# Two heads' scores in single tiles, and unused matmuls in TensorE's waits, at the start of an attention and feed-forward kernel

## The chip, the cores and the metric

The kernel runs on one core of a Trainium2 chip. A core has five engines that run side by side and meet through semaphores: TensorE (PE, matrix products; PEld is its weight load), VectorE (DVE), ScalarE (ACT), GpSimd (POOL) and SyncE (SP), which here only issues transfers. The metric is the time of one execution on the device, in microseconds (us), lower is better. "Before" was run five times: median 357.24, from 355.94 to 357.76.

## The reference

Attention over 8 batches of 8 heads with 576 positions of width 64, then a feed-forward layer. Sixteen beacon keys and values stand ahead of the 576 of each head; every query sees all beacons, and the keys up to its own position.

```python
k_all = np.concatenate([beacon_k, k], axis=2)      # (8, 8, 592, 64)
v_all = np.concatenate([beacon_v, v], axis=2)
scores = scale * np.matmul(q, k_all.transpose(0, 1, 3, 2))
scores = np.where(causal, -1000000000.0, scores)
a = np.exp(scores - scores.max(-1, keepdims=True))
a /= a.sum(-1, keepdims=True) + 1e-09
attn_out = np.matmul(a, v_all)
x = attn_out.transpose(0, 2, 1, 3).reshape(B * S, H * D)   # (4608, 512)
h = x @ w_in                                               # (4608, 2048)
out = np.maximum(0.01 * h, h) @ w_out                      # (4608, 512)
```

## The kernel before, in words

**Pairs.** Heads are worked on two at a time: a pair `g` is batch `g // 4`, heads `2 * (g % 4)` and the next, so there are 32 pairs. For a pair the kernel needs queries and keys transposed (`qT`, `kT`, 128 partitions: two heads of 64), makes the scores as keys by queries in four tiles (`score(g, 0)` to `score(g, 3)`, L286), each followed by one exponential on ScalarE (L306) that writes `aT`, sets the masked part of `aT` to zero on GpSimd (`masks`, L310, four instructions), multiplies by the values (`value(g, 0)` and `value(g, 1)`, L332; a column of ones beside the values gives the sum to divide by), and turns the result (`x_transposes`, L368) into `xT`, where it waits for the second stage. Score tiles have two PSUM buffers of their own (`ps_sc`), so the third tile waits for the first one's exponential. Everything else in PSUM shares four buffers (`ps_one`).

**Two ways to get qT and kT.** Pairs 0 to 7, the first two batches, are transposed by TensorE (`t_q(g, 0)` for queries, `t_q(g, 1)` for keys, L228: 18 transposes each, then a copy, on VectorE or, where the call says so, on ScalarE). The pair after is always prepared while a pair is worked on. From pair 8 on GpSimd reorders the raw data (`permute`, L157), a transposing DMA turns it (`turn_pairs`, L257, issued by SP), and GpSimd copies it in order into `qT` and `kT` (`in_order`, L269 to L282; the copies are L277).

**Second stage.** Rows of `x` are taken in 9 chunks of 512. `moe1` (L382) makes one of 16 tiles of `h` with four matmuls of 512 columns and a leaky ReLU on ScalarE; `moe2` (L398) makes a quarter of an output tile of 128 rows, also four matmuls; every fourth one ends in a copy to `osb` on VectorE and a store issued by SP (L420). `fill()` (L425) emits one such unit, `moe1` or `moe2` by turns, when a chunk is ready. Units are put between the steps of attention so that TensorE has work.

**Transfers.** SP issues the values (`load_v`, L206, six transfers per batch) and the stores; GpSimd issues queries, keys and weights (`load_qk`, `load_w_in`, `load_w_out`). The very first pair is loaded in float32 by SP and ScalarE (`load_first_pair`, L144) and cast by VectorE (queries, L471) and ScalarE (keys, L472). Values are cast to bfloat16 by GpSimd (`cast_v`, L221).

**Order.** The order of instructions on each engine is written out by hand: within `tc.manual_schedule` (L451) every engine executes in the order of the program, and waits in that order. So the loop at L534 is the schedule: in step `g` come `loads(g)`, then, for the first eight pairs (L538 to L562), two score tiles, the transposes of an earlier pair's result, the transposes for the pair to come, the first half of an earlier pair's values, two score tiles, second half, masks. Step 8 (L564) brings the loads of batch 2, the rest of pairs 5 to 7 and a run of 22 units; from there each step has a number of units worked out from what is left (L591 to L597). Before all this `warm_up(34)` (L440, called at L477) issues 34 matmuls of the identity with itself, whose result nobody reads, while the first loads are under way.

Of the kernel before, what the change touches and what calls it, by code (L numbers as in the profile page):

```python
# [8 lines left out]
FP32 = mybir.dt.float32  # L9
# [6 lines left out]
def kernel(  # L16
# [11 lines left out]
    nc = tc.nc  # L28

    B, H, S, D = q.shape  # L30
# [5 lines left out]
    NPAIR = H // 2  # L36
# [41 lines left out]
    ps_one = ctx.enter_context(tc.tile_pool(name="ps_one", bufs=4, space=bass.MemoryType.PSUM))  # L78
# [3 lines left out]
    ident = singles.tile([128, 128], BF16, name="ident")  # L82
# [59 lines left out]
    first_raw = []  # L142
# [78 lines left out]
    def cast_v(b, eng, c0=0, c1=NKB):  # L221
        t, dst = v_raws[b], v_bufs[b % 2]
        for c in range(c0, c1):
            eng.tensor_copy(out=dst[0 : ROWS[c], c, :, 0:D], in_=t[0 : ROWS[c], c])  # L224
# [212 lines left out]
            turn[0] = 0  # L437
        return can1 or can2

    def warm_up(n):  # L440

        ps = ps_one.tile([128, 512], FP32, name="av", tag="one")
        for i in range(n):
            nc.tensor.matmul(out=ps[:, 0:128], lhsT=ident, rhs=ident, start=True, stop=True)

    NG = B * NPAIR

# [12 lines left out]
    with order:  # L460
# [8 lines left out]
        make_ones()  # L469
        cast_beacon_k(0, 1, nc.scalar.copy)  # L470
        nc.vector.tensor_copy(out=first_cast[0], in_=first_raw[0])  # L471
        nc.scalar.copy(out=first_cast[1], in_=first_raw[1])  # L472
        cast_beacon_k(1, B, nc.gpsimd.tensor_copy)
        cast_v(0, nc.gpsimd, 0, 1)
        load_qk(1, 0)
        cast_v(0, nc.gpsimd, 1, 3)
        warm_up(34)  # L477
        beacon_transposes(0, 1)
        t_q(0, 0)
        t_q(0, 1, nc.scalar.copy)  # L480

        def loads(g):
            b, hp = divmod(g, NPAIR)
# [42 lines left out]
        def finish(g):  # L526

            x_transposes(g)
            ready[0] = chunks_with(g)
            if g % NPAIR == NPAIR - 1:  # L530
                turn[0] = 1


        for g in range(NG + 3):  # L534
            if has(g) and g != 2 * NPAIR:
                loads(g)

            if g < 2 * NPAIR:  # L538

                score(g, 0)  # L540
                score(g, 1)
                if has(g - 3):
                    finish(g - 3)
                if g == 2:
                    beacon_transposes(1, B)
                if g + 1 < 2 * NPAIR:
                    t_q(g + 1, 0)
                    t_q(g + 1, 1, nc.scalar.copy if g in (4, 6) else nc.vector.tensor_copy)
                if g > 2:
                    value(g - 2, 0)  # L550
                if g == 7:
                    fill()
                score(g, 2)
                score(g, 3)
                if g == 2:
                    value(0, 0)
                if g >= 6:
                    fill()
                if has(g - 2):
                    value(g - 2, 1)  # L560
                masks(g)
                continue  # L562

            if g == 2 * NPAIR:  # L564

                load_qk(2, 1)
                for grp in range(2):
                    for which in range(2):
                        permute(2, grp, which)
                    turn_pairs(2, grp)  # L570
                load_v(2)
                in_order(g)
                cast_v(2, nc.gpsimd)
                finish(g - 3)
                value(g - 2, 0)
                fill()
                value(g - 2, 1)
                fill()
                finish(g - 2)
                value(g - 1, 0)  # L580
                fill()
                value(g - 1, 1)
                fill()
                fill()
                finish(g - 1)
                for n in range(22):
                    fill()
                loads(g)


            chunks = chunks_with(g - 3) if g - 3 >= 2 * NPAIR else ready[0]  # L591
            groups = 2 * NF * chunks - done1[0] - done2[0]
            steps = NPAIR - (g - 2) % NPAIR if g > 2 * NPAIR + 5 else 2 * NPAIR + 6 - g
            n = -(-(groups - 1) // steps)
            slots = [0] * 8
            for i in range(n):
                slots[(2, 5, 1, 6, 0, 4, 3, 7)[i % 8]] += 1  # L597
            owed = [0]

            def slot(n):  # L600
                owed[0] += slots[n]
                while owed[0] and fill():
                    owed[0] -= 1

            if has(g):
                score(g, 0)
                score(g, 1)
            slot(0)
            if g - 3 >= 2 * NPAIR:
                finish(g - 3)  # L610
            slot(1)
            if g - 2 >= 2 * NPAIR and has(g - 2):
                value(g - 2, 0)
            slot(2)
            slot(3)
            if has(g):
                score(g, 2)
                score(g, 3)
            slot(4)
            if g - 2 >= 2 * NPAIR and has(g - 2):  # L620
                value(g - 2, 1)
            slot(5)
            slot(6)
            if has(g):
                masks(g)
            slot(7)
# [32 lines left out]
```

The softmax here doesn't subtract the row's maximum and nothing guards it: scores larger than these inputs give would overflow.

## Time and profile before

The profiled execution took 357.62 us; its span, from the first to the last instruction, is 355.9 us.

| what | value |
|---|---|
| median of five runs | 357.24 us |
| profiled execution, its span | 357.62 us, 355.9 us |
| busy, share of the span | PE 96%, PEld 49%, POOL 57%, ACT 53%, DVE 26% |
| matmuls L387 (`moe1`), L409 (`moe2`) | 140.2 us, 139.6 us |
| exponentials L306 | 128 in 104.4 us, 869 ns each |
| masks L320 | 128 in 52.5 us, 449 ns each on average |
| read from and written to HBM | 37.22 MB, 9.44 MB |

A line of the timeline gives the start, the length, the engine, the line of the code, the operation, what it writes and reads, the size, and in brackets how long the engine was idle ahead of it and what ended that. A "q" after an engine's name means its queue, as in SPq. In a row of busy times by stage the numbers are, after the stage and its length, the busy us of PE, PEld, DVE, ACT and POOL with the count of instructions, then the granted clock of TensorE as a share of the full one, the mean busy share of the 16 DMA engines (above 1 where packets overlap) and GB/s. The chain of waits is followed back from the last instruction to what released each one. The digits of the clock and of DMA are tenths in 40 equal slices of the span.

### The profile page before, as it was taken

Reading aid. Unit: us, or ns where it says so; the run is one execution under the profiler, and the core shown is the slowest. Engines: PE = TensorE matmul, PEld = TensorE weight load, DVE = VectorE, ACT = ScalarE, POOL = GpSimd, SP = SyncE. Lnnn points to the kernel's source line nnn. Section 1 sums busy time; section 2 is a strip of 40 time slices with the busy share of each in tenths; the row PEclk is TensorE's granted clock in tenths of the full one; section 3 lists DMA queues with packets and bytes.
Section 4 is the critical chain, followed back from the end, with each engine's and each line's share of the span. In section 5 each row is a group of like instructions: output and inputs, shape, how many; then the busy total and the mean of one; then the engine's idle time right before and its main releaser. Section 6 shows DMA issues by size and latency. Waiting matters only on the chain.

```text
span 355.9 us, 7340 instructions
## 1 busy us (share of the span) xinstructions
PE 341.0 (96%) x3002; PEld 172.8 (49%) x3002; DVE 93.9 (26%) x231; ACT 189.3 (53%) x278; POOL 202.0 (57%) x343
## 2 busy tenths in 40 slices
PE   5899999999799999999999999999999999999996
PEld 5566554444344444444444454444444554444444
DVE  2388430102234113311232223222322241000111
ACT  3969754576354873378337843686348403733300
POOL 7599928398799899957695769574441100000000
PEclk9579999999999999999999999999999999999999
DMA  8998999996897985993589455900110011000012
GB/s 166 210 219 135 199 205 201 224 211 88 177 189 118 162 167 98 165 215 49 97 140 213 74 98 100 190 2 1 61 59 2 0 62 59 2 29 29 31 59 88
DMA packets 86929, 40.87 MB, mean 115 GB/s; under 512 B 69872, under 2 KB 82160, under 8 KB 86896
## 3 DMA queue, kind: packets, MB, share of 16 engines
q1 hardware_dynamic: 73456, 26.75, 35.3%
q0 software_dynamic: 13152, 13.34, 24.7%
q8 instruction: 23, 0.38, 0.5%
q10 hardware_dynamic: 288, 0.33, 0.4%
q14 instruction: 10, 0.08, 0.1%
HBM read 37.22 MB, written 9.44 MB: 131 GB/s over the span
## 4 chain that ended last, share of the span: by engine, by line
PE 72%; DMA 11%; POOL 8%; SPq 3%; issue 2%; ACT 2%; DVE 2%; POOLq 0%
PE acc L409 31%; PE acc L387 27%; PE av L351 6%; PE sc L297 6%; DMA v_raw<-in_v_dram 4%; DMA w_out_sb<-in_moe_w_out_dram 4%; DMA q_raw<-in_q_dram 2%; SPq L215 2%; POOL aT L320 2%; DMA v_raw<-in_k_dram 1%; PE tp L373 1%; ACT aT L306 1%; POOL kT L277 1%; POOL qT L277 1%; DVE osb L418 1%
## 5 line engine op out<-in xcount | busy, mean ns | idle before, releaser
L387 PE MATMUL acc<-xT,w_in_sb 128*128 128x512 bf16 x576 | 140.2, 379 | 1.4 <-DVE xT L378 1.4
L409 PE MATMUL acc<-w_out_sb,gT 128*128 128x512 bf16 (+1 forms) x592 | 139.6, 374 | 0.0
L306 ACT ACTIVATE aT<-sc 128x1024 bf16<-128x1024 f32 (+3 forms) x128 | 104.4, 869 | 65.5 <-PE sc L297 65.3
L394 ACT ACTIVATE gT<-acc 128x512 bf16<-128x512 f32 x144 | 85.9, 601 | 79.2 <-PE acc L387 79.2
L409 PEld LDWEIGHTS <-gT 128*128 128x128 bf16 x592 | 53.3, 98 | 58.7 <-issue 6.1
L387 PEld LDWEIGHTS <-w_in_sb 128*128 128x128 bf16 x576 | 51.9, 98 | 59.5 <-issue 4.2
L320 POOL TENSOR_SCALAR_AFFINE_SELECT aT<-aT 128x384 bf16<-128x384 bf16 (+2 forms) x128 | 52.5, 449 | 49.7 <-PE av L351 39.7
L418 DVE COPY osb<-acc 128x512 f32<-128x512 f32 (+1 forms) x37 | 25.1, 677 | 134.7 <-PE acc L409 134.6
L351 PEld LDWEIGHTS <-aT 128*128 128x128 bf16 (+1 forms) x960 | 37.5, 99 | 14.7 <-issue 2.8
L297 PE MATMUL sc<-qT,kT 64*128 64x80 bf16 (+4 forms) x384 | 37.2, 296 | 6.1 <-POOL kT L277 2.9
L351 PE MATMUL av<-v_aug,aT 128*128 128x65 bf16 (+1 forms) x960 | 40.7, 196 | 0.0
L361 DVE TENSOR_TENSOR x_nat<-av,rec 128x384 bf16<-128x384 f32 x64 | 31.4, 491 | 2.2
L224 POOL CAST v_aug<-v_raw 128x512 bf16<-128x512 f32 (+1 forms) x40 | 23.2, 619 | 9.7 <-DMA v_raw<-in_v_dram 9.7
L297 PEld LDWEIGHTS <-kT 64*128 64x128 bf16 x384 | 12.8, 96 | 31.8 <-issue 18.3
L277 POOL COPY qT<-q_turn 128x576 bf16<-128x576 bf16 x24 | 28.1, 1169 | 0.0
L277 POOL COPY kT<-k_turn 128x576 bf16<-128x576 bf16 x24 | 28.0, 1168 | 0.0
L378 DVE COPY xT<-tp 128x576 bf16<-128x576 bf16 x32 | 14.5, 454 | 51.2 <-PE tp L373 51.2
L360 DVE RECIPROCAL rec<-av 128x6 f32<-128x6 f32 x64 | 12.0, 187 | 58.6 <-PE av L351 58.6
L135 POOL DMA_DIRECT2D k_raw<-in_k_dram x31 | 19.4, 625 | 4.5 <-DMA q_raw<-in_q_dram 2.8
L135 POOL DMA_DIRECT2D q_raw<-in_q_dram x31 | 19.0, 613 | 3.1 <-DMA w_out_sb<-in_moe_w_out_dram 3.0
L164 POOL COPY q_nat<-q_raw 128x1152 bf16<-128x1152 bf16 x12 | 13.8, 1147 | 6.5 <-DMA q_raw<-in_q_dram 6.5
L373 PEld LDWEIGHTS <-x_nat 128*128 128x128 bf16 (+2 forms) x160 | 11.2, 98 | 9.3 <-DVE x_nat L361 2.2
(36 smaller groups left out, 86.8 us busy)
## 6 DMA issues: line engine op xcount, KB each, us to landing
out_dram<-osb SPq DMA_DIRECT2D x35, 256.0 KB, 2.3
v_raw<-in_v_dram SPq DMA_DIRECT2D x24, 256.0 KB, 5.2
q_raw<-in_q_dram POOLq DMA_DIRECT2D x31, 144.0 KB, 5.1
k_raw<-in_k_dram POOLq DMA_DIRECT2D x31, 144.0 KB, 5.3
w_in_sb<-in_moe_w_in_dram POOLq DMA_DIRECT2D x4, 512.0 KB, 7.5
w_out_sb<-in_moe_w_out_dram POOLq DMA_DIRECT2D x4, 512.0 KB, 12.6
v_raw<-in_v_dram SPq DMA_DIRECT2D x8, 224.0 KB, 3.9
v_raw<-in_v_dram SPq DMA_DIRECT2D x8, 160.0 KB, 5.2
```

What stands on the lines that cost most here:

```text
L135: dma = nc.gpsimd.dma_start(out=dst[e * RP : (e + 1) * RP], in_=src[b, h0 : h0 + 2].rearrange("h (p i) d -> p h i d", i=RI),)
L224: eng.tensor_copy(out=dst[0 : ROWS[c], c, :, 0:D], in_=t[0 : ROWS[c], c])
L277: nc.gpsimd.tensor_copy(out=dst.rearrange("c (p i) -> c p i", i=RI), in_=t[:, :, e].rearrange("c i p -> c p i"),)
L297: nc.tensor.matmul(out=sc[:, par, col - c0 : col - c0 + w], lhsT=kT[ps_, c * 128 : (c + 1) * 128], rhs=qT[ps_, q0 : q0 + w], start=True, s ...
L306: nc.scalar.activation(out=aT[:, :, c0 : c0 + w], in_=sc[:, :, 0:w], func=AF.Exp, scale=0.125)
L320: nc.gpsimd.affine_select(out=part, in_=part, compare_op=ALU.is_ge, fill=0.0, base=base, channel_multiplier=-1, pattern=pattern,)
L351: nc.tensor.matmul(out=avv[:, n, 0 : D + 1], lhsT=aT[0 : ROWS[c], par, a0 : a0 + 128], rhs=va[0 : ROWS[c], c, 2 * hp + par, :], start=(c = ...
L361: nc.vector.tensor_tensor(out=x_nat[:, t0:t1].rearrange("p t e d -> p (t e) d"), in0=avv[:, :, 0:D], in1=rec[:, n0:n1, None].to_broadcast( ...
L387: nc.tensor.matmul(out=acc, lhsT=w_in_sb[:, j, fc * 128 : (fc + 1) * 128], rhs=xT[:, j, i * 512 : (i + 1) * 512], start=(j == 0), stop=(j ...
L394: nc.scalar.activation(out=gT[i][:, fc, :], in_=acc, func=AF.Prelu, alpha=0.01)
L409: nc.tensor.matmul(out=acc[:, 0:w], lhsT=gT[i][:, fc, t * 128 : (t + 1) * 128], rhs=w_out_sb[:, fc, c0 : c0 + w], start=(fc == 0), stop=(f ...
L418: nc.vector.tensor_copy(out=osb[:, 0:w], in_=acc[:, 0:w])
```

## The change

Five things change, all in the first two batches:

- The cast of the first keys is split: ScalarE casts the first head, VectorE the second.
- `warm_up` becomes `keep_busy`: one PSUM buffer is kept for it, and it is called again, with 12 matmuls each, after the beacon transposes, after the first queries' transposes and after the first keys' transposes, and with 4 to 10 matmuls at several places in steps 0 to 3: 138 more in all. Their results are not read.
- In steps 0 to 7 the third score tile now comes between the query transposes and the key transposes of the next pair, and the fourth after the first half of the values. The beacon transposes of batches 1 to 7 move from step 2 to step 1.
- GpSimd casts the second chunk of the first values before it issues `load_qk(1, 0)`, and not after.
- Step 8 starts with one `fill()` more. The number of units in all is the same; steps 8 to 11 have one fewer between them.

```diff
-    def warm_up(n):
-
-        ps = ps_one.tile([128, 512], FP32, name="av", tag="one")
+    busy = []
+
+    def keep_busy(n):
+
+        if not busy:
+            busy.append(ps_one.tile([128, 512], FP32, name="av", tag="one"))
         for i in range(n):
-            nc.tensor.matmul(out=ps[:, 0:128], lhsT=ident, rhs=ident, start=True, stop=True)
+            nc.tensor.matmul(out=busy[0][:, 0:128], lhsT=ident, rhs=ident, start=True, stop=True)
...
         nc.vector.tensor_copy(out=first_cast[0], in_=first_raw[0])
-        nc.scalar.copy(out=first_cast[1], in_=first_raw[1])
+        nc.scalar.copy(out=first_cast[1][:, 0], in_=first_raw[1][:, 0])
+        nc.vector.tensor_copy(out=first_cast[1][:, 1], in_=first_raw[1][:, 1])
         cast_beacon_k(1, B, nc.gpsimd.tensor_copy)
-        cast_v(0, nc.gpsimd, 0, 1)
+        cast_v(0, nc.gpsimd, 0, 2)
         load_qk(1, 0)
-        cast_v(0, nc.gpsimd, 1, 3)
-        warm_up(34)
+        cast_v(0, nc.gpsimd, 2, 3)
+        keep_busy(34)
         beacon_transposes(0, 1)
+        keep_busy(12)
         t_q(0, 0)
+        keep_busy(12)
         t_q(0, 1, nc.scalar.copy)
+        keep_busy(12)
...
                 score(g, 0)
+                if g < 4:
+                    keep_busy(8)
                 score(g, 1)
                 if has(g - 3):
                     finish(g - 3)
-                if g == 2:
-                    beacon_transposes(1, B)
                 if g + 1 < 2 * NPAIR:
                     t_q(g + 1, 0)
+                if g < 4:
+                    keep_busy((10, 10, 10, 4)[g])
+                score(g, 2)
+                if g + 1 < 2 * NPAIR:
                     t_q(g + 1, 1, nc.scalar.copy if g in (4, 6) else nc.vector.tensor_copy)
                 if g > 2:
                     value(g - 2, 0)
+                elif g == 1:
+                    beacon_transposes(1, B)
+                else:
+                    keep_busy(8)
                 if g == 7:
                     fill()
-                score(g, 2)
                 score(g, 3)
+                if g < 2:
+                    keep_busy(10)
...
                 in_order(g)
                 cast_v(2, nc.gpsimd)
+                fill()
                 finish(g - 3)
```

## The prediction

> **What bounds the kernel now.** I read the page first: TensorE is busy 96% of the span, so the first question is where it isn't, and what it is doing when it looks busy.
>
> The slices of the page, then busy time by stage (each engine's busy us, the granted clock, the DMA share and GB/s):
>
> ```profile
> PEclk9579999999999999999999999999999999999999
> 69.50:104.50 35.00, 32.07 (x268) 14.71 (x265) 8.46 (x19) 20.44 (x29) 31.18 (x51) 1.00 0.91 172
> 104.50:352.00 247.50, 246.07 (x1902) 120.10 (x1903) 57.06 (x136) 124.37 (x188) 122.25 (x202) 1.00 0.43 85
> ```
>
> The clock is halved only early (in slices of 1 us: 0.50 from 9 to 22, 0.67 in the next). From 104.5 on TensorE idles 1.4 us in 247: that stretch is pure TensorE. Between 69.5 and 104.5 it idles 2.9 us. The timeline of TensorE says on what:
>
> ```profile
> 68.19 0.58 PE L297 MATMUL sc<-qT,kT 64*128 64x512 bf16 x4
> 89.86 0.59 PE L297 MATMUL sc<-qT,kT 64*128 64x512 bf16 x4 [1.71 <-POOL kT L277]
> 97.77 0.59 PE L297 MATMUL sc<-qT,kT 64*128 64x512 bf16 x4 [1.20 <-POOL kT L277]
> 104.50 0.59 PE L297 MATMUL sc<-qT,kT 64*128 64x512 bf16 x4
> ```
>
> These are the first scores of pairs 8, 11, 12 and 13. TensorE stands waiting for GpSimd (POOL) to put keys in order. So whatever is gained before 89.86 must also make GpSimd earlier, or it is waited away there. The chain of waits (start, length, what) shows what drives GpSimd:
>
> ```profile
> 20.76 9.06 DMA v_raw<-in_v_dram
> 29.88 0.61 POOL v_aug L224
> ...
> 37.27 12.69 DMA w_out_sb<-in_moe_w_out_dram
> 50.25 7.35 DMA q_raw<-in_q_dram
> ...
> 64.22 5.27 DMA v_raw<-in_v_dram
> ```
>
> No step of scores or exponentials stands in it between 15 and 89 us: transfers and GpSimd follow each other. The GpSimd timeline in the stage of the change:
>
> ```profile
> 12.62 0.62 POOL L224 CAST v_aug<-v_raw 128x512 bf16<-128x512 f32 x1 [3.79 <-DMA v_raw<-in_v_dram]
> 13.18 0.59 POOL L135 DMA_DIRECT2D q_raw<-in_q_dram  x1
> ...
> 16.62 1.63 POOL L320 TENSOR_SCALAR_AFFINE_SELECT aT<-aT 128x224 bf16<-128x224 bf16 x4
> ...
> 29.88 0.61 POOL L224 CAST v_aug<-v_raw 80x512 bf16<-80x512 f32 x1 [0.53 <-DMA v_raw<-in_v_dram]
> ```
>
> From 12.6 to 29.3 it is busy 16.67 of 16.70 us (the fifth number of the stage's row), and never waits for ScalarE. The of pairs 0 to 7 start at 16.6, 19.3, 23.2, 27.2, 31.9, 35.7, 38.8, 42.7, the exponentials they read end at 12.4, 16.0, 20.5, 25.6, 29.8, 33.5, 37.2, 41.6. Faster exponentials make no mask earlier; exponentials 1.1 us late make none later.
>
> **What the skill says.** "TensorE: Matmul & The Clock Gate", Part 1: the clock halves after an idle window of about 3.4 us and returns after a busy one; the trace agrees in kind (half speed for about 13.6 us after the thin stretch 5 to 9, where TensorE was busy 1.62 of 4 us). Part 4 says transposes don't count as busy; no view isolates that, but the half clock did last through 9 to 13 with TensorE busy 3.37 of 3.90. Part 1 prices a 128-column matmul at 107 ns cold and 56 warm; the trace's 34 at the start took 3.81 us, 112 each, and 512 columns at full clock take 0.865/4 = 216, a quarter of it 54. "Trainium Kernel Development and Optimization", Key Constraints: all queues share the same 16 DMA engines and interleave; the trace has 200 GB/s from 45 to 57.6 whoever issued.
>
> **The change, part by part.** (a) First keys in two halves: ScalarE's cast took 1.15 us, a half some 0.6; VectorE's half some 0.4 (q_cast, the same shape, took 0.75). Keys land at 6.24, so the transposes may start near 6.85 instead of 7.46. VectorE now waits for the keys from 5.80 to 6.24, and behind it stand bkT, qT and kT's first columns: qT ends near 7.8 instead of 7.13. The transposes stand behind 12 unused matmuls, to 7.15; kT is copied at 8.3, first score 8.35 instead of 8.67: gain 0.3.
>
> (b) 138 more unused matmuls: 36 before the first score, then 36, 28, 26, 12 in pairs 0 to 3. At 56 ns, 7.7 us; at 112, 15.5. What hides them: 4.6 us of idle TensorE between 5 and 30 (the stage rows' sum), and about 6 us that its 12.6 busy us at half clock lose if the clock stays. So at full clock they fit.
>
> (c) Order and moved transposes. Pair 2 now needs 0.75 (scores) + 0.7 (transposes) + 1.46 (26 x 56 ns) + 1.24 (values) = 4.15 us; its exponentials began at 16.16, the next at 21.69, 5.5 us. Gain 1.4, pairs 0, 1 and 3 a few tenths. Then the masks cap it: values of pair 5 started at 38.24 and their masks end at 37.34; of pair 7 at 45.32, masks end at 44.34. TensorE gets 1.0 us ahead there and no more.
>
> (d) One unit of the second stage (four 512-column matmuls, 0.87 us) earlier, before pair 5's transposes: no work added, it covers a 0.57 us wait at 41.7. With it TensorE is 1.9 us of work ahead at 45, and reaches pair 8's first score near 67.2 instead of 68.19.
>
> (e) What that is worth at 89.86: nothing. Keys of pair 11 are ready at 89.81; the idle time grows from 1.7 to 3.6. The end moves only with GpSimd's own chain, which two things touch.
>
> (f) Second value chunk cast before load_qk(1,0). It was issued at 7.12 and landed 6.4 later, at 13.5, so GpSimd waits 0.35 more; the four issues go from 13.18 to 14.1, masks of pair 0 from 16.62 to 17.05, and everything behind is 0.4 late up to the wait for the last chunk of batch 1, 0.53 long. There the 0.4 vanishes if that chunk still lands at 29.82. It shares engines with the delayed keys: bounds 29.8 to 30.2; I take 0.2 late. From there the loads of weights run back to back to 57, so 0.2 stays.
>
> (g) SP queue. The second output store now stands ahead of load_v(3), because its unit comes before pair 8. VectorE copied that output at 69.78 in before; now near 67.2, stored at 67.95. So load_v(3) goes at 68.45 instead of 67.59, behind a store that no longer competes with load_qk(3,0) later (issued 73.04, waited for by GpSimd 1.98 us until 81.3). Ahead of that transfer: 0.86 us x 0.21 MB more values, 0.26 MB less store. Bounds: 1.0 us late (all values in its way) to 1.25 early (0.256 MB at 205 GB/s); I take 0.3 early.
>
> Sum against the span of 355.9: +0.2 - 0.3 = -0.1, TensorE's gains worth 0. The profiled execution took 357.62, 0.4 over the median 357.24; I apply the difference to the median: 357.1.
>
> **Rivals.** *Faster by a transfer:* if (g) gives its whole 1.25 us (GpSimd could use it: it waits 1.98 and then 1.79 on these loads, and TensorE has slack), 355.8, a little less if (f) costs nothing. For it: the key packets of 75 to 81 share with a store that landed 8.6 us after issue. Against: the third store moves into the freed place. *Slower by the unused matmuls:* if the clock halves although they are there, the 90 of pairs 0 to 2 cost 10 us at 112 ns where TensorE idled 1.2 us from 9 to 21. It decides when exponentials are later than GpSimd's slack (2.7 us at pair 2, 1.6 at pair 3, 1.1 at pair 7): one half-speed window, 1.7 us, is still nearly hidden; four cost about 10 - 1.2 - 2.7 - 1 = 5 us: 362. Against: 34 such matmuls raised the clock at the start. *Slower by transfers:* (f) 0.4 late and (g) 1.0 late: 358.6; the point is TensorE's lead: under 1 us at pair 8, load_v(3) slips by about 2. *TensorE decides after all:* if the waits at 89.86 and 97.77 were on data that come earlier, its 1.9 us of lead would reach the end: 355.3; the start of GpSimd's cast at 65 to 69.5, held by arrivals of values, speaks against.
>
> **Chances.** No change to speak of 0.53 (own range 356.3 to 358.2); faster by transfer or by lead 0.26; slower by transfers 0.13; halved clock 0.08. A measurement of this kernel tells about 0.3% from no change, 1.1 us. The range runs from 355.2, which takes in nearly all faster cases, to 359.0, past slower transfers; the halved clock and tails stay out.
>
> **What would show it.** Right: granted clock 1.00 from 9 to 22; scores of pair 3 near 19.9 instead of 20.97; masks starts unmoved to 0.4 us; the cast at 29.9 still the chain's; idle before pair 11's scores grown to about 3.6 us; pair 13's scores at 104.5 within half a microsecond. Wrong: weight loads on GpSimd at 30.4 or its wait for keys at 81.3 moved by over 1 us, a clock of 0.5 with pair 2's masks waiting for ScalarE, or TensorE after 104.5 idling more than 1.4 us.

## The result: 0.4% slower

| | before | after |
|---|---|---|
| median | 356.98 us (79 runs) | 358.55 us (44 runs) |
| ratio, 95% interval | 1 | 1.0038, 1.0027 to 1.0048 |
| profiled execution, its span | 357.62, 355.9 us | 358.67, 357.0 us |
| first score of pair 13 to the end of the span | 251.4 us | 251.4 us |

The forecast of no change was wrong: the kernel is slower by 0.38%, some 1.4 us; 358.55 lies in the range given, on the side that got 0.21. (The ratio leaves out executions that were disturbed on the chip; the medians are of all.) The last row says where to look: from pair 13's scores on (104.50 before, 105.55 after) both kernels take the same 251.4 us, so all 1.05 us of difference between the two profiles arises ahead of that. In the profiles of all the later runs the stretch is 251.4 us as well (251.9 in one, keys_first).

**Profile after.** The clock of the page and the busy times by stage:

```profile
PEclk9999999999999999999999999999999999999999
12.60:29.30 16.70, 16.61 (x359) 12.00 (x357) 11.13 (x25) 13.04 (x17) 15.30 (x31) 1.00 1.10 183
69.50:104.50 35.00, 31.67 (x266) 14.54 (x265) 8.45 (x19) 21.04 (x30) 31.06 (x52) 1.00 0.89 179
104.50:352.00 247.50, 246.05 (x1898) 119.45 (x1897) 56.88 (x136) 124.40 (x189) 123.19 (x203) 1.00 0.43 86
```

The unused matmuls did what they can do: the clock is full throughout (before, 0.50 from 9 to 22), and TensorE is busy 16.61 of 16.70 us at the start. But GpSimd, the fifth number of a stage, is busy only 15.30 of 16.70 us there, where it was busy 16.67. TensorE's first scores of pairs 8, 11, 12 and 13, from its timeline:

```profile
69.68 0.58 PE L297 MATMUL sc<-qT,kT 64*128 64x512 bf16 x4
...
91.16 0.59 PE L297 MATMUL sc<-qT,kT 64*128 64x512 bf16 x4 [2.37 <-POOL kT L277]
...
98.82 0.58 PE L297 MATMUL sc<-qT,kT 64*128 64x512 bf16 x4 [0.96 <-POOL kT L277]
...
105.55 0.59 PE L297 MATMUL sc<-qT,kT 64*128 64x512 bf16 x4
```

It still waits for GpSimd's keys, longer at pair 11 (2.37 us, 1.71 before), and every one of the four comes 1.0 to 1.5 us later. The chain of waits looks quite different now, and must be read with care:

```profile
20.79 1.03 PE av L351 x30
28.31 0.87 ACT aT L306
...
50.75 6.05 PE acc L387 x28
...
79.20 1.10 POOL qT L277
80.63 1.99 issue
82.64 1.15 POOL q_nat L164
```

Up to 75 us it follows TensorE nearly throughout. That need not mean that TensorE holds the end up: at pair 11 it stands waiting for GpSimd all the same. With unused matmuls in the gaps it has hardly an idle moment at which the chain could step over to another engine. GpSimd's own timeline says what GpSimd waits for:

```profile
13.99 1.20 POOL L224 CAST v_aug<-v_raw 128x512 bf16<-128x512 f32 x2 [5.08 <-DMA v_raw<-in_v_dram]
15.14 0.59 POOL L135 DMA_DIRECT2D q_raw<-in_q_dram  x1
...
18.02 1.64 POOL L320 TENSOR_SCALAR_AFFINE_SELECT aT<-aT 128x224 bf16<-128x224 bf16 x4
...
30.15 1.16 POOL L224 CAST v_aug<-v_raw 128x512 bf16<-128x512 f32 x2
31.26 1.51 POOL L109 DMA_DIRECT2D w_in_sb<-in_moe_w_in_dram  x2
...
44.61 0.59 POOL L135 DMA_DIRECT2D k_raw<-in_k_dram  x1 [1.65 <-DMA w_in_sb<-in_moe_w_in_dram]
45.20 0.86 POOL L320 TENSOR_SCALAR_AFFINE_SELECT aT<-aT 128x224 bf16<-128x224 bf16 x2
...
82.64 1.15 POOL L164 COPY q_nat<-q_raw 128x1152 bf16<-128x1152 bf16 x1 [1.23 <-DMA q_raw<-in_q_dram]
```

The first value cast, at 12.62 before, starts at 13.99: it waits 5.08 us for the first chunk instead of 3.79. All its waits are for transfers, none for TensorE or ScalarE. The delay can be followed: 1.40 us at the masks of pair 0 (16.62 to 18.02); 0.82 at the weight loads (30.44 to 31.26), since the old wait of 0.53 for the last chunk of batch 1 is gone; 2.50 at the masks of pair 7 (42.70 to 45.20), since the last load of batch 2's first keys now waits 1.65 for the weights; 1.6 to 2.0 from 45 to 57, where the next loads wait for weights; 1.31 at 82.64, where the wait for batch 3's keys has shrunk from 1.98 to 1.23; 1.06 at the keys of pair 13 (ready at 104.44, now 105.50). So the delay doesn't simply run on: of the 1.40 only 0.82 are left at 31 us, and the rest is new. The second load of `w_in`, asked for 0.82 late, landed 2.50 late (39.28, before 36.78).

Why is the first chunk late? Its load (L213) was issued at 6.54 (6.64 before). The view of this load has 5.9 us from issue to landing before, and after:

```profile
DMA to landing us min/median/max: 7.3/7.3/7.3
```

A transfer is cut over 16 DMA engines, and each reports its part. "DMA: Bandwidth & Descriptors" of the Trainium skill, section "Why a DMA increments its semaphore by 16 and not by 1", says that the semaphore counts these parts, so a waiter goes on with the last. The 16 times, from the trace's records (us):

```
         parts 1 ... 15 of the first chunk   part 16   first instruction packet of TensorE
before   11.32 ... 12.28                     12.49     11.94 to 13.23
after    11.60 ... 12.20                     13.87     10.91 to 11.90
```

Fifteen parts land as early as before; one is 1.7 us behind them. The weight load named above shows the same: its last part came 2.2 us behind the other fifteen (0.85 before). The other column is the page's queue "q8 instruction": packets of 16,384 bytes, 23 in the run before, 24 after. TensorE has about 6,000 instructions before (matmuls and weight loads on the page) and 276 more after, so some 260 go into a packet, by this estimate. A packet takes 0.9 to 1.5 us. The 36 unused matmuls ahead of the first scores are 72 instructions with their weight loads; in the changed kernel the first packet comes a microsecond earlier, ahead of the first chunk's landing and no longer in the middle of it. That it lies on one DMA engine and holds up that engine's sixteenth is an inference: the trace doesn't say which engine a packet or a part used. It is the theory that the last experiments test; it came only after three others had been tried.

### The profile page after: what moved, and what is told of

Its sections match the earlier page's. It is cut to its first block, busy times and chain, and to the rows that moved or that the text cites. A ratio compares the mean times of both kernels' runs of the same rounds, so it can differ in the third digit from the quotient of the medians.

```text
span 357.0 us, 7618 instructions
## 1 busy us (share of the span) xinstructions
PE 346.4 (97%) x3140; PEld 178.2 (50%) x3140; DVE 94.8 (27%) x232; ACT 189.2 (53%) x278; POOL 201.8 (57%) x343
## 4 chain that ended last, share of the span: by engine, by line
PE 90%; POOL 4%; DVE 2%; issue 2%; ACT 1%; POOLq 0%; ACTq 0%
PE acc L409 34%; PE acc L387 33%; PE av L351 8%; PE sc L297 8%; PE av L447 4%; PE tp L373 2%; PE tp L247 2%; DVE osb L418 1%; ACT aT L306 1%; POOL aT L320 1%; POOL kT L277 1%; POOL k_raw L135 1%; DVE xT L378 1%; POOL qT L277 1%; POOL q_raw L135 1%
## 5 line engine op out<-in xcount | busy, mean ns | idle before, releaser
L351 PEld LDWEIGHTS <-aT 128*128 128x128 bf16 (+1 forms) x960 | 36.7, 98 | 14.6 <-issue 2.8
L297 PE MATMUL sc<-qT,kT 64*128 64x80 bf16 (+4 forms) x384 | 36.3, 284 | 4.1 <-POOL kT L277 3.3
L447 PE MATMUL av<-ident 128*128 128x128 bf16 x172 | 14.0, 239 | 1.4 <-POOL ident masks.py:199 1.4
```

Source lines behind the costliest of these rows:

```text
L297: nc.tensor.matmul(out=sc[:, par, col - c0 : col - c0 + w], lhsT=kT[ps_, c * 128 : (c + 1) * 128], rhs=qT[ps_, q0 : q0 + w], start=True, s ...
L351: nc.tensor.matmul(out=avv[:, n, 0 : D + 1], lhsT=aT[0 : ROWS[c], par, a0 : a0 + 128], rhs=va[0 : ROWS[c], c, 2 * hp + par, :], start=(c = ...
L447: nc.tensor.matmul(out=busy[0][:, 0:128], lhsT=ident, rhs=ident, start=True, stop=True)
```

## The experiments

Ratios are to the kernel before, run beside each experiment (its median 356.5 to 356.9 us), with 95% intervals. The five theories: (1) the moved value cast makes GpSimd late; (2) the unused matmuls slow TensorE down; (3) the extra unit puts a store in front of batch 3's values; (4) TensorE's instruction packet hits the first value chunk, and GpSimd starts late; (5) the new order of score tiles and transposes costs the time.

### Parts of the change, one by one

**undo_cast**: the changed kernel with the order of value casts put back.

```diff
-        cast_v(0, nc.gpsimd, 0, 2)
+        cast_v(0, nc.gpsimd, 0, 1)
         load_qk(1, 0)
-        cast_v(0, nc.gpsimd, 2, 3)
+        cast_v(0, nc.gpsimd, 1, 3)
```

> The changed kernel with the order of GpSimd's first casts and loads as before (one chunk of values, load_qk(1, 0), two chunks). Theory 1, the cast ahead of the loads makes GpSimd's chain of loads late: the whole loss of 0.4% goes, ratio to before 0.998 to 1.001, load_qk(1, 0) issued at 13.2 to 13.9 and not 15.1, first weight load near 26.5 to 27.2 and not 27.8, pair 11's keys in order at 89.5 to 90.2 and not 91.1. Theory 2, the unused matmuls make TensorE late (steps 0 to 3 took 4.4 us each): nothing changes, ratio 1.003 to 1.005. Theory 3, the store ahead of load_v(3): nothing changes, 1.003 to 1.005.

Measured 1.0038 [1.0016, 1.0059], the same loss. The first cast still starts late, at 13.43.

**only_cast**: the kernel before with that edit alone.

> The kernel before with nothing changed but the order of GpSimd's first casts and loads (two chunks of values, then load_qk(1, 0)). Theory 1: the whole loss, ratio 1.003 to 1.005, the second cast ahead of the loads, load_qk(1, 0) about 1 to 2 us later than 13.2, pair 11's keys in order about 1.3 us later than 89.8. Theories 2 and 3: ratio 0.999 to 1.001.

Measured 0.9994 [0.9974, 1.0013]; first cast at 12.39, keys of pair 13 ready at 103.33. Both directions agree: theory 1 falls.

**undo_fill**: the changed kernel without the extra `fill()` at the start of step 8.

> The changed kernel without the one more unit at the start of step 8, so that the second output store stands behind load_v(3) again, as before. Theory 3: the loss goes, ratio 0.998 to 1.001, and GpSimd's wait for the keys of batch 3 near 81 ends about 1 us earlier. Theories 1 and 2: unchanged, 1.003 to 1.005.

Measured 1.0031 [1.0011, 1.0050], not told apart from 1.0038. First cast at 13.59. Theory 3 gets no support, but the test isn't clean: the unit now has to be done between pairs 8 and 11, TensorE takes 19.90 us from one to the other (19.03 in wide, below, which has the unit early), and in this profile it waits for no keys at pairs 11, 12 and 13.

**no_unused**: the changed kernel without the unused matmuls of steps 0 to 3 (those ahead of the first scores stay).

```diff
-                if g < 4:
-                    keep_busy(8)
...
-                if g < 4:
-                    keep_busy((10, 10, 10, 4)[g])
...
-                else:
-                    keep_busy(8)
...
-                if g < 2:
-                    keep_busy(10)
```

> The changed kernel without the 102 unused matmuls of steps 0 to 3 (the 34 at the start and the 36 before the first scores stay). The clock falls to a half again in one of the windows between 9 and 23 us, or stays full. Theory 2: TensorE's steps 0 to 3 shrink by 1 to 2 us in sum and the end comes earlier by as much, ratio 0.997 to 1.000. Theory 1: TensorE isn't what the end waits for, ratio 1.003 to 1.005, idle TensorE before pair 11's scores other than 2.4 us by what it gained or lost before.

Measured 1.0066 [1.0043, 1.0089]: taking them away gains nothing and rather makes it worse, so theory 2 falls for the unused matmuls of steps 0 to 3. Its busy times in the stage of pairs 0 to 3:

```profile
8.50:26.00 17.50, 15.43 (x252) 9.56 (x249) 11.31 (x20) 12.61 (x16) 12.47 (x25) 0.63 1.14 207
```

And its first scores of pairs 11, 12 and 13, from TensorE's timeline:

```profile
91.72 0.58 PE L297 MATMUL sc<-qT,kT 64*128 64x512 bf16 x4
98.72 0.59 PE L297 MATMUL sc<-qT,kT 64*128 64x512 bf16 x4 [0.30 <-POOL kT L277]
105.48 0.59 PE L297 MATMUL sc<-qT,kT 64*128 64x512 bf16 x4
```

The clock falls to 0.63, pair 8's scores come at 72.68, and at pair 11 there is no bracket: TensorE has no slack left there, and 0.30 us at pair 12. So in the new order the unused matmuls seem to earn something; and the first cast is late here too (14.20). In all four profiles of kernels with the 36 unused matmuls ahead of the first scores it was late, in only_cast it wasn't. That led to theory 4.

### The instruction packet

**tiny**: the kernel before with 36 unused matmuls of 64 x 64 at the three places where the change puts its first 36, and nothing else.

```diff
         beacon_transposes(0, 1)
+        tiny(12)
         t_q(0, 0)
+        tiny(12)
         t_q(0, 1, nc.scalar.copy)
+        tiny(12)
```

> The kernel before with 36 unused matmuls of 64 rows by 64 columns, about 25 ns each, 12 at each of the three places where the change has its first ones; nothing else of the change. They add 72 instructions to TensorE's stream and next to no work, so TensorE asks for its next 16 KB of instructions earlier. Theory 4, that fetch occupies one of the DMA engines for 1 to 1.3 us and, when it comes before the first chunk of values has landed, holds one sixteenth of it up, so that GpSimd's chain starts late: fetch at 10.8 to 11.3 instead of 11.9, first chunk cast at 13.4 to 14.2 instead of 12.6, ratio 1.002 to 1.005. Theory 5, the order of score tiles and transposes costs the time, and theory 3, the store ahead of load_v(3): ratio 0.999 to 1.001.

Measured 1.0086 [1.0058, 1.0113]. The packet came at 11.10, the first cast at 14.23: as theory 4 had it. But the loss is more than twice that of the changed kernel and above the forecast, and why isn't known: the profiled execution took 364.17 us where the median is 360.54, so only its start is read here.

**wide**: the changed kernel with 9, 4, 3, 2 or 1 unused matmuls of 512 columns in place of 34, 12, 10, 8 or 4 of 128: about the same TensorE time in a quarter of the instructions.

```diff
-        for i in range(n):
-            nc.tensor.matmul(out=busy[0][:, 0:128], lhsT=ident, rhs=ident, start=True, stop=True)
+        for i in range({34: 9, 12: 4, 10: 3, 8: 2, 4: 1}[n]):
+            nc.tensor.matmul(out=busy[0].rearrange("p (r c) -> p r c", r=4), lhsT=ident,
+                rhs=ident[:, None, :].to_broadcast([128, 4, 128]), start=True, stop=True)
```

> The changed kernel with each four of its unused matmuls of 128 columns made one of 512 (9 at the start, then 4, 3, 2 or 1): about the same TensorE time, some 260 instructions fewer, so that the fetch comes after the first chunk has landed. Theory 4: fetch near 13 or later, first chunk cast at 12.4 to 12.8, pair 11's keys in order at 89 to 90, ratio 0.997 to 1.000, better than the changed kernel by 0.3 to 0.5%. Theories 3 and 5: 1.003 to 1.005, as the changed kernel.

Measured 1.0025 [1.0008, 1.0041]: packet at 13.49, first cast at 12.52, as theory 4 had it; but the ratio is above its forecast and not told apart from 1.0038. A first chunk on time doesn't by itself undo the loss. First scores come at 9.62, 1.3 us later than in the changed kernel, and at pair 11 (90.37) TensorE doesn't wait for keys.

**early_before** and **early_after**: `load_qk(1, 0)` issued ahead of the first value casts, in the kernel before and in the changed one, so that it can't wait for the chunk.

> The kernel before with load_qk(1, 0) issued ahead of all casts of values, in the 3.8 us in which GpSimd waits for the first chunk. All theories have GpSimd's chain of casts, masks and loads as what sets the end: masks of pair 0 about 2 us earlier (near 14.6), the first weight load near 24.5 instead of 26.4. If the chain is GpSimd's own time, ratio 0.994 to 0.998; if the transfers have no room (values land later by what the keys take), 0.999 to 1.003, with the casts waiting for the second, third and last chunks.

> The changed kernel with load_qk(1, 0) issued ahead of all casts of values. Theory 4: the late first chunk now delays three casts but no loads of queries and keys, so most of the 0.4% is back or more, ratio 0.995 to 1.000. If TensorE's own pace in the first steps is what is lost (theory 2 or 5): 1.003 or more, with TensorE not idle before the scores of pair 11.

Measured 1.0057 [1.0035, 1.0080] and 1.0080 [1.0053, 1.0108]: above every forecast for early_before, and above theory 4's for early_after. In early_before the third chunk's cast starts at 19.11 instead of about 16, and the masks of pair 0 at 19.68 (16.62): the keys now land among the values. So this order is worse for both kernels and says nothing for theory 4; the intervals of the two overlap.

**tiny85**: as tiny, with 20, 40 and 25, meant to push the packet to 9 us, clear of the first chunk.

> The kernel before with 85 unused matmuls of 64 by 64 in the same three places (20, 40, 25), so that TensorE asks for its instructions some 2 us earlier still. Theory 4 (the fetch holds up the first chunk of values on one DMA engine): the fetch comes near 9, ahead of that chunk's packets, the first cast is back at 12.4 to 12.8, and the ratio to before is 0.999 to 1.003, better than with 36 (1.0086), although there are more of them; the second fetch may hit a later chunk. If the unused matmuls cost time in another way, more of them cost more: 1.009 or above.

Measured 1.0038 [1.0017, 1.0059]. The packet came at 10.19, not 9, and the first cast at 13.71: the dose was missed, and no clear case came of it. (The profiled execution took 360.44 us, the median is 357.80.) That 85 small matmuls lose no more than 36 fits a loss that doesn't grow with their number.

**wide2**: as wide, but the first 12 unused matmuls, ahead of the first queries' transposes, left at 128 columns.

```diff
-        keep_busy(12)
+        keep_busy(12, False)
```

> The changed kernel with unused matmuls of 512 columns for each four of 128, except the 12 ahead of the first queries' transposes. Theory 4: fetch near 13, first cast at 12.4 to 12.8, 0.998 to 1.002, better than the changed kernel by 0.2 to 0.6%. Theory 3 or 5 alone: 1.003 to 1.005.

Measured 1.0014 [0.9999, 1.0030]. GpSimd's start:

```profile
12.48 0.62 POOL L224 CAST v_aug<-v_raw 128x512 bf16<-128x512 f32 x1 [3.66 <-DMA v_raw<-in_v_dram]
13.46 0.62 POOL L224 CAST v_aug<-v_raw 128x512 bf16<-128x512 f32 x1 [0.36 <-DMA v_raw<-in_v_dram]
14.02 0.59 POOL L135 DMA_DIRECT2D q_raw<-in_q_dram  x1
...
16.90 1.64 POOL L320 TENSOR_SCALAR_AFFINE_SELECT aT<-aT 128x224 bf16<-128x224 bf16 x4
```

With the packet at 12.33 the chunk lands at 12.4, the wait for the second chunk is 0.36, where step (f) of the prediction had put 0.35, and the masks are 0.28 late instead of 1.40. All five edits are in this kernel; with fewer TensorE instructions it loses 0.14% and not 0.38%, some 60% less, though the two intervals just touch.

**wide2_undo_fill**: wide2 without the extra `fill()`.

> The same without the one more unit at the start of step 8, so that load_v(3) stands ahead of the second output store again. If the store and the order of SP's queue cost what is left after the fetch is out of the way: better than with the unit by 0.1 to 0.3%, ratio 0.997 to 1.000, keys of batch 3 waited for about 0.3 us less near 81. If not, equal to it within 0.1%.

Measured 1.0025 [1.0001, 1.0049], no better than wide2: a second test of theory 3, again nothing, and again TensorE takes 19.89 us from pair 8 to pair 11 and waits for no keys.

**keys_first**: the kernel before with the loads of batch 2's keys ahead of the last weight loads.

```diff
             elif g == 6:
-                load_w_out(2)
-                load_w_out(3)
-            elif g == 7:
                 load_qk(2, 0)
+            elif g == 7:
+                load_qk(2, 1)
...
-                load_qk(2, 1)
+                load_w_out(2)
+                load_w_out(3)
```

> The kernel before with the loads of batch 2's queries and keys issued ahead of the last two quarters of w_out (load_qk(2, 0) in step 6, load_qk(2, 1) in step 7, w_out 2 and 3 at the start of step 8). If the end is set by GpSimd and the transfers up to pair 13, as the prediction had it: batch 2 is in order some 3 to 5 us earlier (pair 8 near 58), TensorE's 2.9 us of waiting at pairs 11 and 12 shrink, ratio 0.992 to 0.997. If TensorE's own work sets it, or if w_out comes too late for its first use near 59: 0.999 or more, with TensorE waiting for w_out.

Measured 1.0114 [1.0091, 1.0137], slower where a gain was expected: TensorE reaches pair 8 only at 73.72, and none of the first scores of pairs 8 to 13 waits for keys. TensorE is late, but not by its own work: its longest wait on the way, 3.6 us, is for GpSimd's masks, which start at 48.00 for pair 7 (42.70 before).

### What a late GpSimd costs, and what the order costs

**pool_late**: the kernel before with GpSimd's two memsets of `make_ones()` again, behind the first cast.

> The kernel before with make_ones() called a second time between GpSimd's first value cast and load_qk(1, 0): some 1.1 us more on GpSimd and nothing else. Theory 4 (a late GpSimd start is the loss): the start of load_qk(1, 0) comes about 1.1 us later; the 0.53 us wait at the last chunk of batch 1 takes up part, so the mask of pair 13 is ready about 0.5 us late and the ratio is near 1.0015. If a late start counts whole, kT of pair 13 is 1.1 us late and the ratio 1.003, which would leave nothing of the loss for the order of the score tiles. If the delay is absorbed altogether (ratio 0.999 to 1.001), a late chunk on GpSimd can't be the cause and theory 4 falls.

Measured 0.9987 [0.9972, 1.0001], but `load_qk(1, 0)` was issued only 0.20 us later (13.38): the transfers' issue ran beside the memsets. A missed dose, and no evidence.

**pool_late2**: the first cast done four times, which does hold GpSimd.

```diff
-        cast_v(0, nc.gpsimd, 0, 1)
+        for _ in range(4):
+            cast_v(0, nc.gpsimd, 0, 1)
```

> The kernel before with GpSimd's first value cast done four times over instead of once: three more casts of 0.56 us, so load_qk(1, 0) and everything behind it on GpSimd start 1.7 us late, and nothing else is changed. In pool_late the added memsets took only 0.2 us of GpSimd, so its result said little. Theory 4 (a GpSimd that starts late is the loss): load_qk(1, 0) at 14.9 us as in the changed kernel (15.1), keys of pair 13 ready about 1 us late, ratio 1.002 to 1.005. If it is within 0.999 to 1.001, the late start isn't the cause and the loss must come from what the unused matmuls do to TensorE or to later transfers.

Measured 1.0034 [1.0019, 1.0049]. GpSimd's timeline:

```profile
12.90 2.66 POOL L224 CAST v_aug<-v_raw 128x512 bf16<-128x512 f32 x4 [3.73 <-DMA v_raw<-in_v_dram]
15.51 0.59 POOL L135 DMA_DIRECT2D q_raw<-in_q_dram  x1
...
18.97 1.63 POOL L320 TENSOR_SCALAR_AFFINE_SELECT aT<-aT 128x224 bf16<-128x224 bf16 x4
```

and TensorE's first scores of pairs 11 to 13:

```profile
91.25 0.58 PE L297 MATMUL sc<-qT,kT 64*128 64x512 bf16 x4 [0.79 <-POOL kT L277]
98.83 0.59 PE L297 MATMUL sc<-qT,kT 64*128 64x512 bf16 x4 [0.87 <-POOL kT L277]
105.57 0.59 PE L297 MATMUL sc<-qT,kT 64*128 64x512 bf16 x4
```

Not an instruction of TensorE is touched, yet these three starts are those of the changed kernel to 0.1 us (91.16, 98.82, 105.55), and the ratio is too. The dose is somewhat larger than the changed kernel's (load_qk(1, 0) 2.33 us late against 1.96, masks 2.35 against 1.40); by 75 us both are 2.1 late. A GpSimd that starts 2.3 us late is enough for the whole loss: this is shown, whatever makes it late. That 1.4 us at the masks would be enough isn't.

**tiny_late**: tiny's 36 matmuls in steps 1 to 3, 12 in each, after the first packet.

> The kernel before with the same 36 small unused matmuls as tiny, but 12 each in steps 1, 2 and 3 instead of ahead of the first scores. Theory 4: the first instruction fetch stays near 11.9 us, the first value chunk lands at 12.5, and the ratio is 0.999 to 1.002. If it is 1.005 or more as in tiny (1.0086), the small matmuls cost by themselves wherever they stand.

Measured 1.0043 [1.0025, 1.0061], half of tiny's loss and more than expected. The first packet stayed at 12.54, but the chunk was late all the same:

```profile
13.38 0.62 POOL L224 CAST v_aug<-v_raw 128x512 bf16<-128x512 f32 x1 [2.63 <-DMA v_raw<-in_v_dram]
```

One of its 16 parts came at 13.26, the other fifteen by 12.24, and in this execution one part had lagged by about a microsecond since 7.75, with no packet recorded that accounts for it. So there is at least one other way in which the chunk can be late, and small unused matmuls may cost something besides.

**order_only**: the kernel before with only the new order of score tiles, transposes and values. **wide2_old_order**: wide2 with the old one.

> The kernel before with the new order of score tiles, transposes and values in the first two batches and nothing else: no unused matmuls, one cast of the first keys, the old order of value casts. Theory 4: the first chunk lands at 12.5 us as before, so no more than 0.1% of loss (ratio 0.999 to 1.001). If the order itself costs what is left when the fetch is out of the way: 1.0015 to 1.003, with the scores of pair 8 later than 68.2 us.

> The kernel with 512-wide unused matmuls (few instructions, first chunk at 12.4 us), but with the score tiles in the order of the kernel before. If the order costs what is left: 0.998 to 1.000, below the 1.0014 of the same kernel with the new order. If the rest is the extra unit of work or the unused matmuls themselves: 1.001 to 1.003, no different from it.

Measured 1.0019 [0.9995, 1.0043] and 1.0031 [1.0013, 1.0049]. The first interval holds no change. The second kernel should have gained and did not; its first chunk came late (cast at 13.66) though its packet came at 12.23, again with one part lagging beforehand, since 9.65. Whether the order costs 0.1 or 0.2% isn't settled.

All profiles together (first cast and first packet in us; the profiled execution of each kernel):

```
first packet before 11.6:  after 13.99, undo_cast 13.43, undo_fill 13.59, no_unused 14.20,
                           tiny 14.23, early_after 14.35, tiny85 13.71
first packet from 11.9 on: before 12.62, only_cast 12.39, wide 12.52, early_before 12.62, wide2 12.48,
                           wide2_undo_fill 12.42, keys_first 12.40, pool_late 12.69, order_only 12.60,
                           weights_first 12.64, pool_late2 12.90;  wide2_old_order 13.66, tiny_late 13.38
```

Seven of seven are late in the first row, two of thirteen in the second. One of the seven is no case for the packet: in undo_fill two parts lagged by about a microsecond from 7.5 on, four microseconds before the packet, as one did in tiny_late and wide2_old_order. In the other seventeen profiles no part is more than 0.5 us behind the fifteen others until the packet, and the first that is lands 2.5 to 4.2 us after the packet's start, 0.6 to 2.1 us behind (loads of queries, keys and values):

```
first packet      transfer that is first to have a late part     profiles
10.19 to 11.28    first chunk of values                          after, undo_cast, no_unused, tiny, early_after, tiny85
11.94 to 12.60    third chunk                                    before, only_cast, wide2, wide2_undo_fill, keys_first,
                                                                 pool_late, order_only, weights_first, pool_late2
12.73             first load of load_qk(1, 0)                    early_before
13.49             fourth chunk                                   wide
```

So the kernel before has its late part too, only in a chunk that GpSimd casts later: the third lands at 15.25 there and is cast from 16 on. When the packet moves, the late part moves with it. That makes the packet the likely cause of the late chunk in the changed kernel, though not the only possible one: I couldn't move the packet alone.

What a late chunk costs is seen less sharply in these single executions. Among the profiles but those named below, pair 13's first scores come at 103.1 to 104.5 where the first cast was on time (seven profiles, 103.9 on average) and at 104.0 to 105.6 where it was late (six, 105.0). That is 1.1 us on average, less than the spread within either group (1.4 and 1.5). (Left out are tiny and tiny85, whose executions were long, and the five kernels that move GpSimd's loads or hold it up: early_before, early_after, keys_first, weights_first and pool_late2.)

### A version that is faster than both

**weights_first**: the kernel before with the loads of `w_in` ahead of the value casts of batch 1 in steps 3 and 4. The idea comes from the same reading: GpSimd's issue order sets the end, and its casts held the weight loads back.

```diff
             elif g == 3:
-                cast_v(1, nc.gpsimd, 0, 3)
                 load_w_in(0)
+                cast_v(1, nc.gpsimd, 0, 3)
             elif g == 4:
-                cast_v(1, nc.gpsimd, 3, 5)
                 load_w_in(1)
                 load_w_in(2)
+                cast_v(1, nc.gpsimd, 3, 5)
```

> The kernel before with the loads of w_in of batch 0 and 1 issued on GpSimd ahead of the value casts of batch 1 in steps 3 and 4. If GpSimd's casts and DMA issues of the first batches set the end, the weights land about 1 to 2 us earlier and the last load_qk no longer waits for them, and the time falls by 0.5 to 1.5 us (ratio 0.996 to 0.999). If the transfers' total sets it, no change (0.999 to 1.001).

Measured 0.9973 [0.9955, 0.9991], 356.10 us. GpSimd's timeline:

```profile
24.77 0.79 POOL L109 DMA_DIRECT2D w_in_sb<-in_moe_w_in_dram  x1
...
28.77 1.51 POOL L109 DMA_DIRECT2D w_in_sb<-in_moe_w_in_dram  x2
30.27 1.18 POOL L224 CAST v_aug<-v_raw 128x512 bf16<-128x512 f32 x2
```

TensorE's first scores of pairs 11 to 13:

```profile
89.37 0.59 PE L297 MATMUL sc<-qT,kT 64*128 64x512 bf16 x4
96.02 0.59 PE L297 MATMUL sc<-qT,kT 64*128 64x512 bf16 x4
102.66 0.59 PE L297 MATMUL sc<-qT,kT 64*128 64x512 bf16 x4
```

The weights are asked for 1.64 and 1.67 us earlier, the 0.53 wait at the last chunk is gone, and the keys of pair 13 are ready at 102.47 instead of 104.44. No bracket is left: TensorE goes through all three pairs without waiting. It need not take this edit: in the profile of pool_late, whose GpSimd starts 0.20 us later than before, no bracket is left either, and pair 13 comes at 103.14. So GpSimd is the limit by little more than a microsecond (104.50 against 103.14 at pair 13), and with GpSimd that much earlier TensorE's own gains would count.

## Why the prediction was wrong

**What it had right.** The base: GpSimd and transfers set the end, not TensorE. pool_late2 and weights_first moved the end by moving GpSimd alone. (By a small margin, as pool_late shows.) Step (e), that what TensorE gains ahead of 89.86 is worth nothing, has an answer in the kernel before as well: of 250 executions of it, 97 happened to run at a mean clock of 0.99 or more and took 356.81 us on average; the other 153, with a lower mean clock as in its profile, took 356.83. The difference is 0.02 us, to within 0.23: the half clock that the change removes costs the kernel before nothing that can be seen. Step (a) put the first scores at 8.35 (8.32), and the clock of 1.00 from 9 to 22 came as said.

**The step that failed is (f), with (b) behind it.** Step (f) reckoned only with the later second chunk: load_qk(1,0) at 14.1, masks of pair 0 at 17.05. They came at 15.14 and 18.02. It took for granted that the first chunk still lands at 12.5. It landed at 13.87, 1.4 us that stand in no term of the sum. Step (b) asked of the unused matmuls only whether TensorE has the time for them; that they are also 276 instructions to be fetched, in packets that the page counts among the DMA transfers, was put at nothing without a reason. The number of packets stands on the page (23 on "q8 instruction"), and the trace has the first of them at 11.94, within a microsecond of the chunk that GpSimd waits for. That GpSimd was late by this chunk is measured; that the packet made it late is likely, not shown. How the chunk's delay would go on was reckoned correctly up to one point: 0.53 of it vanished at the last chunk of batch 1. But what was left did not stay the same "back to back to 57": from 0.82 it grew to 1.6 to 2.0 as the weight loads landed later than they were asked for, with one part 2.2 us behind, and it fell to 1.3 at 82.64. What held that part up wasn't tested.

**Steps (b), (c) and (d), TensorE's lead.** The price of one unused matmul was right: within a run they start 55 to 57 ns apart. "TensorE: Matmul & The Clock Gate" of the Trainium skill gives, in its section "Back-to-back issue gap", an isolated gap of 56 and a sustained figure of about 81 for a stream of weight loads and matmuls; this trace has the former. But each run costs about 0.1 us more at its ends: ten take 0.66 us until the next matmul starts, four 0.33. In pair 2 the 26 took 1.76 us in three runs, and not 1.46, and the scores 1.15, and not 0.75 (counted up to the next start). From 8.32 to 26.08 TensorE is busy 17.76 of 17.76 us: the unused matmuls didn't fit into waits, they filled the steps. From pair 2's exponentials to pair 3's were 4.81 us against 4.15 reckoned; pair 3's scores came at 21.76 and not 19.9, pair 8's at 69.68 and not 67.2. The lead of 1.9 us turned into 1.5 of lag. Because of (e) this hurt nobody in the profile of the changed kernel, where TensorE still waits for keys.

**Step (g)** put load_v(3) at 68.45. SP's queue after:

```profile
68.97 1.90 SPq L420 DMA_DIRECT2D out_dram<-osb  x2
70.91 0.42 SPq L210 DMA_DIRECT2D v_raw<-in_beacon_v_dram  x1
```

The store does stand in front, but most of the 3.3 us comes from behind: load_v(2) was itself 2.1 us late (63.81, before 61.69), since SP's queue follows GpSimd. Undoing the extra unit twice changed nothing measurable. The gain of 0.3 that this term stood for is not seen; whether the store costs anything isn't settled, as undoing the unit also gave TensorE more to do.

**The rivals.** "Slower by transfers" had named the right place and even the time, 358.6, at a chance of 0.13, but by the wrong delay (the second chunk and load_v(3) instead of the first chunk and the weights): that its figure fits is luck. "Slower by the unused matmuls" through a halved clock did not happen; "faster by a transfer" would have needed load_v(3) early.

**What stays open.** pool_late2 shows that a late GpSimd start of 2.3 us suffices. That the packet makes GpSimd late in the changed kernel rests on the late part that follows the packet in seventeen profiles, and on wide2. How much of the loss comes from the first chunk, and how much from the late part of the weight loads, wasn't taken apart. What wide2 still loses (0.14%, with an interval that takes in no change; it keeps one PSUM buffer for the unused matmuls too, which no run tests alone), whether the new order costs anything, why tiny loses more than the changed kernel, and why small unused matmuls after the first packet (tiny_late) still cost 0.43% wasn't settled.

## What to carry to other kernels

An instruction that "costs nothing" on its engine still has to be fetched, and the packets show among the DMA transfers. Where a transfer that heads the critical chain lands within some 4 us after such a packet, as the first chunk did here, count instructions, and try few wide matmuls in place of many narrow ones. When a filler keeps an engine busy throughout, the chain of waits stops telling what bounds the kernel; read instead the brackets of the engine that the end waits for. And before a change that speeds up an engine, look for its natural experiment: executions of this kernel that had the higher clock said that it was worth nothing that can be seen.

## What the runs showed of the hardware

- TensorE's instructions arrive in packets of 16 KB, some 260 instructions each by the counts above, one about every 16 us in the second stage here, each 0.9 to 1.5 us long. A cast waits for the slowest sixteenth of its transfer: fifteen parts by 12.20, the last at 13.87, the cast at 13.99.
- In seventeen of twenty profiles the first late part of a transfer landed 2.5 to 4.2 us after the first packet's start, 0.6 to 2.1 us behind the other fifteen.
- In three profiled executions one or two of the sixteen parts lagged by about 1 us for several transfers in a row ahead of the first packet, with no packet of instructions recorded that explains it (from 7.5 in undo_fill, from 7.75 in tiny_late, from 9.65 in wide2_old_order).
- The same kernel has a full clock in some executions and not in others: 97 of 250 executions of the kernel before had a mean clock of 0.99 or more, and 41 of 44 of the changed one. The profile of the kernel before, with a mean of 0.981, has its half clock from 9 to 22 us; those of pool_late and weights_first, without the added unused matmuls, have 1.00 there.
- A memset on GpSimd ran beside the issue of transfers behind it (two memsets, 0.20 us of delay), a cast did not (three more casts and a chunk 0.28 us later, 2.33 us of delay).
